# Batch 0's x moved to SyncE's queue, between pieces of w_in, and the first stage's order rewritten around it

## The chip, the cores and the metric

The kernel runs on one core of a Trainium2 chip. The metric is the device time of one execution in microseconds (us), as the median of several runs.

## The reference

Two blocks follow each other. The first is a cross attention between x (8 batches, 8 heads, 512 tokens, 64 channels) and a state (8, 8, 32, 64), in both directions; the second is a feed-forward layer on the 4352 resulting rows of 512 (8 batches of 512 + 32 tokens).

```python
scores = scale * np.matmul(x, state.transpose(0, 1, 3, 2))      # x reads state
a = softmax(scores); xread = np.matmul(a, state)
scores2 = scale * np.matmul(state, x.transpose(0, 1, 3, 2))     # state reads x
a2 = softmax(scores2); sread = np.matmul(a2, x)
x2 = rows of concat([xread, sread])                             # (4352, 512)
h = x2 @ w_in                                                   # w_in (512, 2048)
out = (h * sigmoid(1.702 * h)) @ w_out                          # w_out (2048, 512)
```

The softmax subtracts the maximum and divides by the sum plus 1e-9. x, state and out are 32-bit floats; w_in and w_out come as 64-bit floats, and the kernel itself makes 32-bit ones of them.

## The kernel before

The order of every instruction on each engine is written by hand: the program is under `manual_schedule`, and each engine works through its instructions in the order of the code. The change lies in the first stage, which brings in the data and handles batches 0 and 1; batches 2 to 7 follow in a different way and are not touched.

**Transfers.** The states of batches 0 and 1 come in two halves (`load_two_states`, L138, 64 KB each, issued from ScalarE's queue); a GpSimd copy makes a second arrangement of each half. `load_x(b)` (L150) brings one batch's x, 1 MB: batch 0's in four pieces of 256 KB from ScalarE's queue, batch 1's in two pieces of 512 KB from SyncE's queue, in rows of 1 KB. `load_weights(upto)` (L272) goes on with the list of weight pieces up to a number; a piece (`load_weight`, L185) is 512 KB of w_in or w_out as 64-bit words, in rows of 4 KB, always from SyncE's queue. Four pieces (NPR = 4) hold a quarter of w_in's columns.

**Making 32-bit weights.** For each piece, VectorE takes the exponent bits (`mask`, L217), two ScalarE activations turn these into a power (`round_a`, L224, driven by `powers_to`, L277), and VectorE takes the fraction (`fraction`, L236), puts the sign to the power (`sign`, L243) and finishes with two products (`round_b`, L248, driven by `round_to`, L283). `round_to(n, ahead)` brings the pieces below n to their end, and the masks and powers of `ahead` more.

**Attention of a batch.** `two_states(b, banks)` (L313) turns the states on TensorE into two PSUM banks and copies them on ScalarE into `pairs`, four copies of 64x128; `state_copies(b)` (L325) makes two further copies of 128x128. `xT_part(b, j)` (L338) turns a quarter of x, that is two heads, with four TensorE transposes and one ScalarE copy to SBUF. `x_scores(b, j, banks)` (L352) makes a quarter of the scores with eight matmuls, from the turned x and `pairs`. `head_max`, `head_sub` (L362, L369, VectorE), `head_exp` (L376, ScalarE), `head_sum` and `head_scale` (L380, L389, VectorE) are the softmax of x's direction; `head_back` (L395) turns its result with eight TensorE transposes, copied by ScalarE. `att_scores(b)` (L412) makes the scores of the other direction and needs the copies of `state_copies`. `att_M(b, c)` (L542) multiplies the states by a quarter of w_in, and `up_x` (L626) makes hidden units of that product and the turned softmax, with the gelu on ScalarE.

**Buffers.** `att_ps` gives a PSUM buffer from psA, of which there are two. `bank_o` are four banks by themselves; `held` is the last two of them, and `apart` two banks of psH. The turned x of the two batches shares one SBUF buffer, and `pairs` is one buffer too.

**Warm-up.** `keep_warm(n, bank)` (L129) issues n bf16 matmuls of 128x512 on zeros, which nothing reads; the result goes to a bank that is not in use then.

Of the kernel before, what the change touches and what calls it, by code (L numbers as in the profile page):

```python
# [10 lines left out]
FP32 = mybir.dt.float32  # L11
# [9 lines left out]
def kernel(  # L21
# [30 lines left out]
    nc = tc.nc  # L52
# [5 lines left out]
    P = 128  # L58
    NPR = P // Ns
    NG = H // NPR  # L60
# [3 lines left out]
    FC = 512  # L64
# [10 lines left out]
    x_four = x.rearrange("b h (q c) d -> b q h (c d)", c=SCH)  # L75
# [13 lines left out]
    psH = ctx.enter_context(tc.tile_pool(name="psH", bufs=2, space=bass.MemoryType.PSUM))  # L89
# [4 lines left out]
    def att_ps(shape, name):  # L94
        return psA.tile(shape, FP32, tag="att", name=name)
# [31 lines left out]
    bank_o = [psO.tile([P, FC], FP32, tag=f"o{i}", name=f"o_{i}") for i in range(4)]  # L127

    def keep_warm(n, bank=None):  # L129
        ps = psH.tile([P, FC], FP32, tag="h", name="warm") if bank is None else bank  # L130
        for _ in range(n):
            nc.tensor.matmul(ps, zeros[:, :P], zeros, start=True, stop=True)


    xn, xsq, stn = {}, {}, {}
    two = [konst.tile([P, 2, 2, D], FP32, name=f"states_{i}") for i in range(2)]

    def load_two_states():  # L138

        for u in range(2):  # L140
            nc.scalar.dma_start(two[0][:, :, u], st_h[:, :2, u])
        for u in range(2):
            nc.gpsimd.tensor_copy(two[1][:, :, 1 - u], two[0][:, :, u])
# [6 lines left out]
    def load_x(b):  # L150
        t = sums[:, 0] if b == 1 else xpool.tile([P, SCH, H, D], FP32, tag="xn", name=f"xn_{b}").rearrange("p c h d -> p (c h d)")
        xn[b] = t.rearrange("p (h c d) -> p h c d", h=H, c=SCH)
        n = NPR if b else NG
        for i in range(H // n):
            h = slice(n * i, n * (i + 1))
            (nc.sync if b else nc.scalar).dma_start(xn[b][:, h].rearrange("p h c d -> p h (c d)"), x_four[b, :, h])

    def load_x_squares(b):
        xsq[b] = xpool.tile([P, NPR, S], FP32, tag="xn", name=f"xsq_{b}")
# [25 lines left out]
    def load_weight(i):  # L185

        key = PIECES[i]
        nin, room = NFC * NPR, NF // 2
        if i < room or nin - NPR <= i < nin:
            o = 2 * (i % room if i < room else i - (nin - NPR))  # L190
            raw[i] = w_out[:, o : o + 2].rearrange("p f n -> p (f n)").bitcast(I32)
        else:
            o = 2 * (i % 4)
            raw[i] = later[:, o : o + 2].rearrange("p f n -> p (f n)").bitcast(I32)
        if key[0] == "i":
            _, c, k = key
            src = w_in_words[P * k : P * (k + 1), 2 * FC * c : 2 * FC * (c + 1)]
        else:
            src = w_out_words[P * key[1] : P * (key[1] + 1)]
        nc.sync.dma_start(raw[i], src)  # L200
# [23 lines left out]
    def round_a(i):  # L224

        if i not in power:
            mask(i)
        sc = power[i]
        if i in (NFC * NPR + 2, NFC * NPR + 3):
            nc.vector.tensor_scalar(sc, sc, most, least, ALU.min, ALU.max)  # L230
            nc.vector.tensor_scalar(sc, sc, -least, 8.0, ALU.add, ALU.mult)
            return
        nc.scalar.activation(out=sc.bitcast(FP32), in_=sc, func=AF.Relu, bias=edge[0], scale=-8.0)
        nc.scalar.activation(out=sc, in_=sc.bitcast(FP32), func=AF.Relu, bias=edge[1], scale=-1.0)
# [37 lines left out]
    def load_weights(upto):  # L272
        while done["load"] < min(upto, len(PIECES)):
            load_weight(done["load"])
            done["load"] += 1

    def powers_to(n):  # L277
        while done["a"] < min(n, len(PIECES)):
            load_weights(done["a"] + 1)
            round_a(done["a"])  # L280
            done["a"] += 1

    def round_to(n, ahead=AHEAD):  # L283

        nin = NFC * NPR
        while done["b"] < min(n, len(PIECES)):
            i = done["b"]
            powers_to(i + 1)
            round_b(i, min(i + 1 + ahead, i + 3 if i > nin + 3 else i + 2 if i >= nin else nin), i >= nin or i + 1 < nin and (i + 1 < n or i >= NPR))
            done["b"] += 1  # L290
            while done["b"] > NPR and done["load"] < len(PIECES) and before(done["load"]) < done["b"]:
                load_weights(done["load"] + 1)
# [20 lines left out]
    def two_states(b, banks):  # L313

        A[b]["turn"] = banks
        A[b]["two"] = [apool.tile([P, P], FP32, tag=f"two{i}", name=f"two{i}_{b}", bufs=2) for i in range(2)]
        for ps, t in zip(banks, two):
            nc.tensor.transpose(ps, t[:, b].rearrange("p u d -> p (u d)"), ident)
        for i in range(2):
            rows = slice(D * i, D * (i + 1))  # L320
            for u in range(2):
                src = banks[u ^ i][rows].rearrange("p (h n) -> p h n", n=Ns)
                nc.scalar.copy(pairs[rows, NPR * u : NPR * (u + 1), i], src)

    def state_copies(b):  # L325
        for t, ps in zip(A[b]["two"], A[b]["turn"]):
            nc.scalar.copy(t, ps)
# [24 lines left out]
    def x_scores(b, j, banks):  # L352

        ps = banks[j // 2].rearrange("p (c g j n) -> p c g j n", c=SCH, g=NG, n=Ns)[:, :, :, j % 2]
        for g in range(NG):
            for i in range(2):
                nc.tensor.matmul(
                    ps[:, 2 * i : 2 * i + 2, g], A[b]["xT"][:, NG * j + g, i], pairs[:, NG * j + g].rearrange("p i n -> p (i n)"),
                    start=True, stop=True,
                )  # L360
# [8 lines left out]
    def head_sub(b, i, banks):  # L369
        a = A[b]  # L370
        t = a["e1"][:, :, :, 2 * i : 2 * i + 2].rearrange("p c g j n -> p (c g) j n")
        ps = banks[i].rearrange("p (k j n) -> p k j n", j=2, n=Ns)
        mx = a["mx"][:, i].rearrange("p (k j) -> p k j", j=2)
        nc.vector.tensor_tensor(out=t, in0=ps, in1=mx.to_broadcast((P, SCH * NG, 2, Ns)), op=ALU.subtract)

    def head_exp(b):  # L376
        t = A[b]["e1"]
        nc.scalar.activation(out=t, in_=t, func=AF.Exp, scale=scale)
# [16 lines left out]
    def head_back(b, g, bank=None):  # L395

        a = A[b]
        if g == 0:
            a["aT"] = low[:, :NG] if b == 1 else apool.tile([P, NG, S], FP32, tag="aT", name=f"aT_{b}")
        ps = att_ps([P, SCH, P], f"aT_{b}_{g}") if bank is None else bank.rearrange("p (c q) -> p c q", c=SCH)  # L400
        for c in range(SCH):
            nc.tensor.transpose(ps[:, c], a["e1"][:, c, g].rearrange("p j n -> p (j n)"), ident)
        nc.scalar.copy(a["aT"][:, g], ps.rearrange("p c q -> p (c q)"))
# [8 lines left out]
    def att_scores(b):  # L412
        a = A[b]
        a["s"] = bank_o[:NG] if b == 0 else bank_o[NG:]
        if b > 1:
            by_state(b, a["s"], lambda rows, j: a["xT"][rows, j])
            return

        for g in range(NG):
            for j in range(NPR):  # L420
                st = slice(Ns * j, Ns * (j + 1))
                for i in range(2):
                    rows = slice(D * i, D * (i + 1))
                    nc.tensor.matmul(
                        a["s"][i][st, 2 * P * g : 2 * P * (g + 1)], state_of(b, NG * j + g, i),
                        a["xT"][rows, NG * j + g], start=True, stop=True,
                    )
# [827 lines left out]


    load_two_states()
    load_x(0)
    load_weights(NPR)
    load_x(1)  # L1260
    load_weights(2 * NPR)
    nc.scalar.activation(out=one, in_=one, func=AF.Exp)
    keep_warm(14)
    powers_to(1)
    fraction(0)
    powers_to(2)
    round_to(2, 0)
    two_states(0, [bank_o[i][:, :P] for i in range(2)])
    held, apart = bank_o[NG:], [psH.tile([P, FC], FP32, tag="h", name=f"apart_{i}") for i in range(2)]
    for j in range(NPR):  # L1270
        keep_warm(1, held[0])
        xT_part(0, j, apart[j - 2] if j > 1 else None)
    for j in range(NPR):
        x_scores(0, j, held)
# [5 lines left out]
    fraction(2)  # L1280
    head_max(0, 1, held)
    head_sub(0, 1, held)
    att_scores(0)
    two_states(1, [att_ps([P, P], f"two_{i}") for i in range(2)])
    state_copies(1)
    xT_part(1, 0)
    head_exp(0)
    keep_warm(1, held[0])
    xT_part(1, 1)
    x_scores(1, 0, apart)  # L1290
    xT_part(1, 2)
    x_scores(1, 1, apart)
    keep_warm(1, held[0])
    xT_part(1, 3)
    x_scores(1, 2, apart)
    round_to(3, 1)
    head_sum(0)
    mask(NPR)
    powers_to(NPR + 1)
    head_scale(0)  # L1300
    for g in range(NG):
        head_back(0, g)
    x_scores(1, 3, apart)
    keep_warm(2, held[0])
    round_to(NPR, 2)
    att_M(0, 0)
    for i in range(2):
# [349 lines left out]
```

## Time and profile before

| | |
|---|---|
| median of 3 runs | 696.64 us (696.45 to 696.75) |
| the profiled execution | 697.09 us |
| its span, first to last instruction | 695.3 us |
| PE busy | 684.9 us, 98% of the span |
| PE weight loads (PEld, beside the matmuls) | 585.3 us |
| VectorE (DVE) busy | 558.4 us, 80% |
| ScalarE (ACT) busy | 325.9 us, 47% |
| DMA from 3 to 28 us | 390 GB/s, 9.74 MB |
| first up_x | 30.8 us |
| granted TensorE clock, mean | 0.996 |

The span runs from the first instruction to the last; the profiled execution's own time lies 1.8 us over it. In the profile L12 means line 12 of the kernel, SPq and ACTq are the issues of transfers on the queues of SyncE and ScalarE, and "out<-in" are the program's buffers. Batch 0's x is `xn`, batch 1's is `sums`, and a piece of w_in arrives in `w_out` or `later`, whose room it borrows.

### The profile page before, as it was taken

To read this page: it belongs to the slowest core of one execution; us is meant where nothing else is said; L and a number is where in the kernel's file an instruction comes from. 1 tells how busy PE (TensorE), PEld (TensorE's weight loads), DVE (VectorE), ACT (ScalarE), POOL (GpSimd) and SP (SyncE) were. 2 spreads that over 40 slices of the span, in tenths; PEclk is the share of its full clock that TensorE was granted. 3 is DMA by queue.
4 is the path that set the end of the run, shared out by engine and by line. 5 is a ranking of instruction groups with operands and counts; after the bars stand their busy time and mean duration, and the time that the engine had idled before them with its cause. 6 is when DMAs were issued, how large, how long until landed. Compare 5 with 4: busy or idle time off the path is not lost.

```text
span 695.3 us, 13727 instructions
## 1 busy us (share of the span) xinstructions
PE 684.9 (98%) x5408; PEld 585.3 (84%) x5408; DVE 558.4 (80%) x1066; ACT 325.9 (47%) x728; POOL 1.9 (0%) x11
## 2 busy tenths in 40 slices
PE   8899999999999999999999999999999999999996
PEld 5543577778998899889988999989988998999995
DVE  4899898999999888788969796988788895886540
ACT  5788844224337523753355534643375236421410
POOL 1000000000000000000000000000000000000000
PEclk9999999999999999999999999999999999999999
DMA  9711336146534564346441755166424740251000
GB/s 323 290 61 62 122 122 140 46 175 194 194 74 127 167 191 147 64 129 194 150 95 48 229 166 114 29 182 203 120 46 138 212 138 16 76 166 46 4 2 29
DMA packets 100160, 87.41 MB, mean 126 GB/s; under 512 B 56576, under 2 KB 79616, under 8 KB 100096
## 3 DMA queue, kind: packets, MB, share of 16 engines
q1 hardware_dynamic: 98464, 85.35, 41.5%
q10 hardware_dynamic: 1632, 1.18, 0.5%
q8 instruction: 43, 0.70, 0.4%
q14 instruction: 21, 0.17, 0.1%
HBM read 68.94 MB, written 17.56 MB: 124 GB/s over the span
## 4 chain that ended last, share of the span: by engine, by line
PE 94%; ACT 3%; DMA 2%; ACTq 0%; DVE 0%; issue 0%; DVEq 0%
PE low L764 28%; PE o L1174 15%; PE o L764 15%; PE upx L1174 6%; PE h L621 5%; PE M L410 4%; PE o L1472 4%; PE down L1472 3%; PE o L663 2%; PE upw L1174 2%; PE o L813 2%; PE down_up L621 2%; DMA xn<-in_x_dram 1%; PE o L410 1%; PE upx_sr L1174 1%; DMA out_dram<-osb_sr 1%
## 5 line engine op out<-in xcount | busy, mean ns | idle before, releaser
L764 PE MATMUL low<-w_out,g_room 128*128 128x128 f32 x416 | 54.3, 276 | 0.0
L764 PEld LDWEIGHTS low<-w_out,g_room 128*128 128x128 f32 x416 | 50.5, 192 | 4.5 <-issue 4.2
L1174 PE MATMUL o<-ta,M 128*128 128x256 f32 x192 | 49.9, 382 | 0.0
L1174 PE MATMUL upx<-aT,M 128*128 128x256 f32 x192 | 49.3, 379 | 0.0
L764 PE MATMUL low<-low,g_room 128*128 128x128 f32 x336 | 43.3, 275 | 0.0
L1174 PEld LDWEIGHTS o<-ta,M 128*128 128x128 f32 x192 | 35.5, 190 | 6.0 <-ACT g_room L1220 1.6
L764 PEld LDWEIGHTS low<-low,g_room 128*128 128x128 f32 x336 | 40.3, 192 | 0.2 <-DVE later L769 0.2
L1174 PEld LDWEIGHTS upx<-aT,M 128*128 128x128 f32 x192 | 36.0, 190 | 4.6
L553 ACT COPY M<-M 128x512 f32<-128x512 f32 x57 | 29.7, 594 | 15.4 <-PE M L410 15.4
L1180 ACT ACTIVATE g_room<-o 128x512 f32<-128x512 f32 (+1 forms) x56 | 31.3, 560 | 10.4 <-PE o L1174 10.4
L764 PE MATMUL low<-sums,later 128*128 128x128 f32 x272 | 34.9, 275 | 0.0
L764 PEld LDWEIGHTS low<-sums,later 128*128 128x128 f32 x272 | 32.7, 192 | 0.1
L820 DVE TENSOR_TENSOR g_room<-g_room 128x512 f32<-128x512 f32 x48 | 31.7, 684 | 0.2
L1174 PE MATMUL o<-ta,ms 128*128 128x256 f32 x120 | 30.8, 379 | 0.0
L621 PE MATMUL h<-aT,M 128*128 128x512 f32 x64 | 28.9, 599 | 0.0
L1220 ACT COPY g_room<-o 128x512 f32<-128x512 f32 (+1 forms) x28 | 15.5, 555 | 25.4 <-PE o L1174 25.4
L1180 ACT ACTIVATE g_room<-g_room 128x512 f32<-128x512 f32 (+1 forms) x28 | 16.8, 600 | 20.8 <-DVE g_room L1183 20.8
L1174 PEld LDWEIGHTS o<-ta,ms 128*128 128x128 f32 x120 | 22.8, 190 | 3.1
L621 PEld LDWEIGHTS h<-aT,M 128*128 128x128 f32 x64 | 11.8, 190 | 15.8 <-issue 11.5
L1174 PE MATMUL o<-aT,m 128*128 128x256 f32 x96 | 24.6, 379 | 0.0
L764 PEld LDWEIGHTS o<-w_out,g_room 128*128 128x128 f32 x160 | 19.4, 192 | 5.0 <-issue 5.0
L410 PE MATMUL M<-w_in,stT 64*32 64x512 f32 x344 | 23.2, 592 | 0.0
(316 smaller groups left out, 1653.6 us busy)
## 6 DMA issues: line engine op xcount, KB each, us to landing
low<-low SPq DMA_DIRECT2D x108, 256.0 KB, 2.6
low<-low SPq DMA_DIRECT2D x11, 768.0 KB, 4.3
later<-in_moe_w_out_dram SPq DMA_DIRECT2D x16, 512.0 KB, 3.5
w_out<-in_moe_w_in_dram SPq DMA_DIRECT2D x12, 512.0 KB, 7.4
xsq<-in_x_dram SPq DMA_DIRECT2D x96, 64.0 KB, 2.3
xn<-in_x_dram SPq DMA_DIRECT2D x12, 512.0 KB, 4.4
out_dram<-osb SPq DMA_DIRECT2D x15, 256.0 KB, 2.2
out_dram<-later SPq DMA_DIRECT2D x14, 256.0 KB, 2.2
```

Of the source, the lines that this page charges most:

```text
L410: nc.tensor.matmul(ps[g][st], state_of(b, NG * j + g, g), rhs(rows, j), start=True, stop=True)
L553: nc.scalar.copy(m[:, g], ps[g])
L621: nc.tensor.matmul(hps, lhs[i], rhs[i], start=(i == 0), stop=(i == n - 1))
L663: nc.tensor.matmul(ps[:, r], lhs[f][:, P * r : P * (r + 1)], rhs[:, f], start=(first and r == 0 and f == 0), stop=(f == HF - 1), skip_grou ...
L764: nc.tensor.matmul(ps, lhs[f], rhs[:, f], start=(first and f == 0), stop=(f == QF - 1), skip_group_check=True)
L813: nc.tensor.matmul(ps[:, r], lhs[f][:, P * r : P * (r + 1)], rhs[:, f], start=(r == 0 and f == 0), stop=(f == HF - 1), skip_group_check=True,)
L820: nc.vector.tensor_tensor(out=out, in0=x0, in1=x1, op=op)
L1174: nc.tensor.matmul(ps[:, k], lhs[i][:, o : o + P], rhs[i], start=(first and k == 0 and i == 0), stop=(i == n - 1), skip_group_check=True,)
L1180: nc.scalar.activation(out=dst, in_=src, func=AF.Gelu_apprx_sigmoid)
L1220: nc.scalar.copy(c12, Y(u))
L1472: nc.tensor.matmul(ps7[name][:, HN * r : HN * (r + 1)], lhs[:, P * r : P * (r + 1)], rhs, start=(i == 0 and r == 0), stop=(i == HF - 1), s ...
```

## The change

All four pieces of batch 0's x are issued from SyncE's queue, after the first two pieces of w_in and before the third. Of the transfers of the first stage only the two of the states stay on ScalarE's queue. The warm-up at the start has 10 matmuls instead of 14, and `two_states(0)` is followed by two; the single warm-ups ahead of each turn of batch 0's x and those among batch 1's turns and scores go. Batch 1's states are turned and copied ahead of `att_scores(0)`, into the two `apart` banks instead of two buffers of psA. `head_exp(0)` comes ahead of the first turn of batch 1's x, and `powers_to(NPR + 1)` behind `head_back(0)`.

```diff
@@ load_x
-            (nc.sync if b else nc.scalar).dma_start(xn[b][:, h].rearrange("p h c d -> p h (c d)"), x_four[b, :, h])
+            nc.sync.dma_start(xn[b][:, h].rearrange("p h c d -> p h (c d)"), x_four[b, :, h])
@@ the first stage
     load_two_states()
+    load_weights(2)
     load_x(0)
     load_weights(NPR)
     load_x(1)
     load_weights(2 * NPR)
     nc.scalar.activation(out=one, in_=one, func=AF.Exp)
-    keep_warm(14)
+    keep_warm(10)
     powers_to(1)
     fraction(0)
     powers_to(2)
     round_to(2, 0)
+    held, apart = bank_o[NG:], [psH.tile([P, FC], FP32, tag="h", name=f"apart_{i}") for i in range(2)]
     two_states(0, [bank_o[i][:, :P] for i in range(2)])
-    held, apart = bank_o[NG:], [psH.tile([P, FC], FP32, tag="h", name=f"apart_{i}") for i in range(2)]
+    keep_warm(2, held[0])
     for j in range(NPR):
-        keep_warm(1, held[0])
         xT_part(0, j, apart[j - 2] if j > 1 else None)
     for j in range(NPR):
         x_scores(0, j, held)
@@
     head_max(0, 1, held)
     head_sub(0, 1, held)
+    two_states(1, [apart[i][:, :P] for i in range(2)])
+    state_copies(1)
     att_scores(0)
-    two_states(1, [att_ps([P, P], f"two_{i}") for i in range(2)])
-    state_copies(1)
+    head_exp(0)
     xT_part(1, 0)
-    head_exp(0)
-    keep_warm(1, held[0])
     xT_part(1, 1)
     x_scores(1, 0, apart)
     xT_part(1, 2)
     x_scores(1, 1, apart)
-    keep_warm(1, held[0])
     xT_part(1, 3)
     x_scores(1, 2, apart)
     round_to(3, 1)
     head_sum(0)
     mask(NPR)
-    powers_to(NPR + 1)
     head_scale(0)
     for g in range(NG):
         head_back(0, g)
+    powers_to(NPR + 1)
     x_scores(1, 3, apart)
-    keep_warm(2, held[0])
     round_to(NPR, 2)
     att_M(0, 0)
```

## The prediction

> **What bounds the kernel now.** I read the chain that ended last first: 94% of it is PE, and in order of time it shows no wait worth a change after 30.9 us, so what can be won at the start lies ahead of that.
>
> ```profile
> 2.26 7.92 DMA xn<-in_x_dram
> 10.22 1.11 PE xT L349 x4
> 11.78 1.11 PE apart L349 x4
> 13.32 0.66 PE apart L349 x4
> 13.97 3.52 PE o L357 x32
> 17.49 1.02 PE o L424 x32
> 18.82 0.42 ACT low L323 x2
> 20.00 0.66 PE xT L349 x4
> 24.56 0.59 ACT xT L350
> 30.88 5.35 PE h L621 x12
> ```
>
> The columns are start, length and what. Batch 0's x is awaited until 10.2, its last pieces keep PE until 14.0, its scores end at 17.4; then batch 1's states pass through ScalarE, then batch 1's x, and at 24.6 the chain changes to ScalarE, which works without a pause up to the first copy of M at 30.1. From 30.8 PE runs on. Next the stretches (core 0; PE, PEld, DVE, ACT, POOL busy, granted clock, DMA share, GB/s):
>
> ```profile
> 0.00:5.00 5.00, 3.81 (x9) 1.35 (x10) 0.28 (x2) 0.00 (x0) 1.24 (x9) 1.00 0.61 188
> 5.00:8.00 3.00, 2.48 (x8) 0.82 (x7) 1.28 (x3) 2.13 (x4) 0.67 (x2) 1.00 1.04 378
> 8.00:9.00 1.00, 0.47 (x3) 0.09 (x3) 0.28 (x1) 1.00 (x2) 0.00 (x0) 1.00 1.11 358
> 10.20:13.60 3.40, 3.37 (x13) 2.28 (x14) 2.99 (x6) 2.31 (x7) 0.00 (x0) 0.50 1.08 355
> 3.00:28.00 25.00, 22.07 (x159) 15.21 (x157) 16.09 (x30) 16.11 (x34) 0.67 (x2) 0.93 1.04 390
> ```
>
> From 3 to 28 us the DMA engines are full at 390 GB/s: nothing arrives sooner unless something else arrives later. So order of arrival is what counts. And PE had half its clock from 10.2 to 13.6. The waits of SyncE's queue and its timeline give the landings:
>
> ```profile
> SPq L156 <- DMA states<-in_state_dram: 2.0, 1, 2.0
> SPq L200 <- DMA xn<-in_x_dram: 1.8, 3, 1.2
> 7.54 0.38 SPq L156 DMA_DIRECT2D sums<-in_x_dram  x1
> 12.93 0.33 SPq L200 DMA_DIRECT2D later<-in_moe_w_in_dram  x1
> ```
>
> [...] batch 1's first x at 7.54 with the second states, the next at 8.97 with the first x of batch 0, then at 10.20, 11.75 and 12.93 with its second to fourth. PE's turns start with these (8.99, 10.22, 11.78, 13.11). Batch 1's two x pieces land by 14.01 and 15.51 in the same way. The first two weight pieces land at 5.19 and 6.71, where VectorE's masks begin.
>
> [...] x, behind the states on ScalarE's queue, lands between pieces of w_in, 1.2 to 1.6 us apart. [...] Here it changes at about 6.8, 10.2 and 13.6. [...] the stretch before 13.6 held 12 turns and two or three warm-up matmuls, and full clock followed.
>
> **The change part by part.**
>
> *x of batch 0 moves to SyncE's queue behind two pieces of w_in.* Ahead of and with its last piece are then 0.13 MB of states, 1.05 MB of w_in and 1.05 MB of x: 2.23 MB. By the stretches the engines had moved 5 x 188 = 0.94 MB at 5 us, 2.07 MB at 8 and 2.43 at 9, so 2.23 MB at about 8.45. Landing lags: by 6.71 about 1.58 MB had moved, while the landed pieces are 1.1 MB, some 1.1 us less. Last piece 8.45 + 1.1 = 9.6 us instead of 12.9; the others at 0.26 MB over 376 GB/s = 0.7 us: 7.4, 8.1, 8.85. Bounds 9.0 to 10.5[...]. Issue costs little: SyncE takes about 0.4 us for each, all six by 3 to 5 us, well before the data can flow. [...]
>
> *What comes later for it.* w_in's third piece lands at 9.6 + 0.52 MB/0.39 = 11.0 (before, about 8.4 at the earliest, used at 12.8 by VectorE), the fourth at 12.3, batch 1's x at 13.8 and 15.3, as before, the same bytes being ahead. VectorE's rounding of the first two pieces ends near 11.2: it used to wait for ScalarE until 8.72, since ScalarE, held by its issues until 5.7, loaded its table at 5.77. Now that load is over by 3.3 and the first power runs at 5.7, not 7.2. So the mask of the third piece (0.42 us) is not held up, and ScalarE's powers of it end at about 13.4.
>
> *States.* [...] second half at 7.0 (bounds 6.5 and 7.54), plus POOL's copy of 0.30: PE turns them at 7.35.
>
> *Warm-up.* 14 took 5.96 us, 0.43 each, thus half clock; 10 end at 1.19 + 4.27 = 5.5. With windows as before, the one ending at 6.8 is then busy for 60%; that from -0.0 to 3.4 was busy 65% and brought no full clock, so PE stays at half. States 0.43, two warm-ups 0.85: 8.65. Turns of x at 4 x 0.21 = 0.85: 9.5, 10.3. The window 6.8 to 10.2 is busy for 2.9 of 3.4 us, 84%[...]. I take full clock at 10.2: turns three and four at 0.45 each end at 11.2. Scores 3.57 (13.81 to 17.38): **14.8 instead of 17.4**, 2.6 us won. ScalarE's four copies of states (0.21 each) and first copies of x fit under these turns.
>
> *Batch 1's states ahead of att_scores, exp ahead of the first copy, no warm-ups.* With S the end of scores: before, turning the states waited for att_scores (0.9), their copies ended at S + 2.6 (20.0), and the turn of x had to wait for their PSUM buffers (1.35), so that scores(1,0) began at S + 3.96. After: states turned at S + 0.3, six copies of 0.21 to S + 1.6; exp needs max and sub of the second half on VectorE (2 x 0.7) and ends at S + 2.6; x's turns have run beside it; its copy 0.55: scores(1,0) at S + 3.2. The copies, scores (0.9) and turns (0.45) that alternate then reach the fourth copy at S + 6.15, against 24.56 - 17.38 = 7.2: **1.0 won**. What waits behind the exp is that copy and PE's scores; they are in this sum.
>
> *powers_to(NPR + 1) behind head_back.* Two activations, 1.4 us, trade places with two copies of aT. From the fourth copy to M, ScalarE has the same sum (three pairs of 1.4, two copies of 0.47), 5.6 us: no gain there, but att_M starts 1.4 earlier and has slack. VectorE's third rounding, which att_M needs, ends after its 0.33 mask, sign, two products (0.6 each) behind the power: about 24.9, before M's copy at 26.6.
>
> Sum: 2.6 + 1.0 = 3.6 us, the first up_x at 27.2. After it, VectorE must follow: at 45.6 it had piece 7 ready (44.2 + 0.69) 0.7 us ahead of PE. Its third rounding moves from 28.9 to 24.9, so it keeps pace. The profiled execution took 697.09 us (span 695.3, 1.8 around it), 0.45 over the median of 696.64; so 693.5 profiled, **693.1 as median**.
>
> **Rivals.**
> 1. *Clock already full when x comes* (windows lying otherwise, one inside the warm-ups): turns limited by landing, 9.6 + 0.6, scores end at 13.8; 4.6 won, 692.0. [...] Against: ten warm-ups span 4.3 us, so a window of 3.4 fits only in a quarter of the positions.
> 2. *Clock full only at 13.6*: 84% did not suffice. Turns end at 12.05, scores do 1.6 us of work at half rate, S = 16.3; 2.1 won, 694.5.
> 3. [...] the gain is given back: x lands no sooner in effect, because its slowest engine lags or VectorE's third rounding slips by 2 to 3 us behind w_in's later pieces, and PE waits at 45.6. Only batch 1's part is left, 1.0 or less: 696.0. Against: 2.2 MB ahead instead of over 3.
> 4. *Slower: the missing warm-ups cost the clock.* If PE counts turns badly, neither 10.2 nor 13.6 nor 17.05 raises it: scores take 7.1 us, S = 19.2, 1.8 late; what follows until 20.5 runs at half as well (0.9 more), less the 1.0: 698.4. It decides where full clock comes after about 17.6 us. Against: the trace's raise at 13.6 after mostly turns, and scores are plain matmuls.
>
> **Numbers.** Likeliest case 0.58, rival 1 0.13, 2 0.15, 3 0.08, 4 0.06. Cases one to three are faster by over 0.2% (1.4 us, about what a measurement of this kernel can tell from no change): 0.86; same 0.08; slower 0.06. The likeliest case with x between 9.0 and 10.5 gives 692.4 to 694.2; the range reaches to rivals 1 and 2: 691.8 to 695.2.
>
> **What would show it.** Right: the last turn of x starting near 10.5, scores ending near 15, batch 1's state copies before att_scores ends, the first up_x near 27.2, no new PE wait at the second att_M. Wrong: turns waiting for DMA beyond 11, a half clock while the scores run, VectorE idle for w_in's third piece, or an up_x start won and lost again before 62 us.

## The result, and the profile after

The changed kernel takes **692.87 us** (median of 4 runs, 692.59 to 693.3) against 696.69 before, measured beside it: ratio 0.9946, 95% interval 0.9929 to 0.9963. The forecast was 693.1 with a range of 691.8 to 695.2. The profiled execution took 692.59 us with a span of 690.8; before, 697.09 and 695.3. The profile of before lies 0.4 us above its median and that of the changed kernel 0.3 below, so the two profiles differ by 4.5 us and the medians by 3.8.

The chain of waits of the changed kernel, its first 31 us (start, length, what):

```profile
3.04 6.06 DMA xn<-in_x_dram
...
9.15 0.67 PE apart L349 x4
9.82 0.11 issue
9.93 0.63 PE apart L349 x4
10.56 3.54 PE o L357 x32
...
15.56 1.06 ACT e L378
16.62 0.48 ACT xT L350
17.11 0.04 issue
17.15 1.10 PE apart L357 x8
...
20.02 0.59 ACT xT L350
...
23.67 0.70 DVE w_in L263
24.38 0.04 issue
24.42 0.62 PE M L410 x2
...
26.33 4.92 PE h L621 x11
```

x of batch 0 is still what the chain starts from, but its third piece lands at 9.1 instead of 11.75, the fourth turn starts at 9.9 instead of 13.1, and the scores run from 10.4. Between them and batch 1's first scores at 17.15 now stand VectorE's maximum and subtraction and ScalarE's exp, and the states of batch 1 have left the chain. Further on the way has changed too: before, ScalarE led without a pause to the first copy of M, and now VectorE's rounding of w_in's fourth piece (the prediction's third rounding), which ends at 24.4, is what att_M waits for (0.36 us). ScalarE is no freer for it: it works without a pause from 20.02 to M's copy at 25.6, and both ways end within some 0.2 us of each other. The first up_x comes 4.5 us sooner (26.3 against 30.8), and PE then works without a wait worth naming, so that the end moves by the same 4.5 us between these two executions.

The stretches of the changed kernel (PE, PEld, DVE, ACT, POOL busy, granted clock, DMA share, GB/s):

```profile
2.26:5.67 3.41, 3.37 (x8) 0.91 (x6) 0.55 (x2) 0.98 (x3) 0.34 (x1) 1.00 0.94 322
5.67:9.09 3.42, 1.90 (x12) 1.33 (x12) 2.61 (x6) 3.28 (x7) 0.32 (x2) 1.00 1.11 349
10.20:13.60 3.40, 3.40 (x34) 3.40 (x32) 2.77 (x5) 3.00 (x7) 0.00 (x0) 1.00 1.05 373
3.00:28.00 25.00, 22.10 (x185) 14.69 (x184) 20.36 (x38) 19.23 (x41) 0.66 (x2) 1.00 1.04 388
```

The DMA engines are as full from 3 to 28 us as before (388 against 390 GB/s): nearly the same bytes in another order. In the same 25 us VectorE is busy for 20.4 instead of 16.1 us and ScalarE for 19.2 instead of 16.1: the work that used to follow has moved in. And the clock from 10.2 to 13.6 is 1.00, not 0.50. In the kernel before, the trace has the granted clock change at 6.81, 10.22 and 13.64, 3.41 us apart; a window means here a stretch of that length from one such place to the next. In this execution full clock began at 5.67, behind a window in which warm-ups kept PE busy for 3.37 us of 3.41 (its line shows 1.00 only because the trace has no record of the clock before its end), and lasted, though PE was busy for only 1.90 us (56%) of the next window.

A wait of SyncE's own queue, changed kernel (waited for: us in total, times, longest):

```profile
SPq L156 <- DMA states<-in_state_dram: 0.9, 1, 0.9
```

Batch 1's x still waits for the second half of the states, but 0.9 us instead of 2.0: it is issued at 7.07, not 7.54. The DMA engines stay full meanwhile (349 GB/s from 5.67 to 9.09).

### The profile page after: what moved, and what is told of

The parts are those of the page before. It is cut to its first block, busy times and chain, and to the rows that moved or that the text cites. A ratio compares the mean times of both kernels' runs of the same rounds, so it can differ in the third digit from the quotient of the medians.

```text
span 690.8 us, 13707 instructions
## 1 busy us (share of the span) xinstructions
PE 680.8 (99%) x5398; PEld 583.5 (84%) x5398; DVE 558.6 (81%) x1066; ACT 325.7 (47%) x728; POOL 1.9 (0%) x11
## 4 chain that ended last, share of the span: by engine, by line
PE 94%; ACT 2%; DMA 2%; DVE 1%; SPq 0%; issue 0%; DVEq 0%
PE low L764 28%; PE o L1174 15%; PE o L764 15%; PE upx L1174 6%; PE h L621 5%; PE M L410 4%; PE o L1470 4%; PE down L1470 3%; PE o L663 3%; PE upw L1174 2%; PE o L813 2%; PE down_up L621 2%; PE o L410 1%; PE upx_sr L1174 1%; DMA out_dram<-osb_sr 1%; PE sr L595 1%
## 5 line engine op out<-in xcount | busy, mean ns | idle before, releaser
L764 PEld LDWEIGHTS low<-low,g_room 128*128 128x128 f32 x336 | 40.3, 192 | 0.2 <-DVE later L769 0.2
L1180 ACT ACTIVATE g_room<-o 128x512 f32<-128x512 f32 (+1 forms) x56 | 31.3, 559 | 10.4 <-PE o L1174 10.4
L1174 PE MATMUL o<-ta,ms 128*128 128x256 f32 x120 | 30.8, 379 | 0.0
## 6 DMA issues: line engine op xcount, KB each, us to landing
w_out<-in_moe_w_in_dram SPq DMA_DIRECT2D x12, 512.0 KB, 10.2
```

Of the source, the lines that this page charges most:

```text
L764: nc.tensor.matmul(ps, lhs[f], rhs[:, f], start=(first and f == 0), stop=(f == QF - 1), skip_group_check=True)
L1174: nc.tensor.matmul(ps[:, k], lhs[i][:, o : o + P], rhs[i], start=(first and k == 0 and i == 0), stop=(i == n - 1), skip_group_check=True,)
L1180: nc.scalar.activation(out=dst, in_=src, func=AF.Gelu_apprx_sigmoid)
```

## The experiments

Theory: x's place in the order of arrival carries some 3 us, batch 1's rewritten order some 1 us, and the clock decides how much of the first is seen. Rivals: the warm-ups carry the gain; the landing of x alone decides; scores raise the clock by themselves.

**The changed kernel again** (no edit), to see its spread.

> The changed kernel once more, to see how its times spread. If the clock at the start is a matter of where the clock's windows lie (theory), its times fall between 692.4 and 694.0, those with full clock from the warm-ups near 692.6 and those with full clock only from 9 to 10 us near 693.3, and the profile may show either. If the spread of the first four runs (0.7 us) was chance of the measurement alone (rival), the times lie as close together as those of the kernel before, within 0.4 us.

Measured: 693.48 (692.80 to 693.79, 5 runs), ratio 0.9952 (0.9940 to 0.9964). Two runs lie at 692.80 and 692.85, three at 693.48 to 693.79; with the four of the first measurement, four of nine lie at or below 692.85, five from 693.11 up, and the median of the nine is 693.11. The mean granted clock goes with it: 0.998 in the four, 0.996 or 0.997 in the five. The profile fell into the upper group. Its stretches between the clock's changes (4.05, 7.46 and 10.88), and its chain:

```profile
0.64:4.05 3.41, 2.86 (x7) 1.03 (x8) 0.28 (x2) 1.49 (x2) 1.03 (x5) 1.00 0.55 152
4.05:7.46 3.41, 1.08 (x5) 0.34 (x3) 1.43 (x4) 1.63 (x3) 0.66 (x2) 1.00 1.08 371
7.46:10.88 3.42, 3.42 (x15) 2.83 (x15) 3.38 (x7) 2.83 (x8) 0.00 (x0) 0.50 1.06 380
```

```profile
8.84 1.71 PE xT L349 x8
10.55 1.09 PE apart L349 x8
11.64 3.54 PE o L357 x32
```

The first stretch was at half clock too, whatever its 1.00 says (its warm-ups take 0.43 us each, those at full clock 0.21); full clock began at 4.05, after a window that was busy for 2.86 of 3.41 us, 84%. It was lost after the next one (1.08 of 3.41), in which the ten warm-ups had run out and the states weren't there, and came back at 10.88. The first eight turns of x take 1.9 us in the timeline, against 1.0 in the first profile, and the scores end 1.1 us later. (The end of the scores, S, is taken here as the start of the next matmul.) For x and the scores that is the case that the prediction called likeliest (S = 14.8, here 15.0); the first profile is its rival 1 (13.8, there 13.9). In these two traces the groups are two places of full clock. Both had it while warm-ups ran (from 5.67 and from 4.05); in one it lasted until x came, in the other it was lost at 7.46 and came back at 10.88.

**The transfers alone.**

```diff
     load_two_states()
+    load_weights(2)
     load_x(0)
...
-            (nc.sync if b else nc.scalar).dma_start(xn[b]...
+            nc.sync.dma_start(xn[b]...
```

> The kernel before with the transfer edit alone: x of batch 0 on SyncE's queue behind two pieces of w_in; warm-ups, batch 1's states, exp and powers as before. Theory (arrival decides): x's last piece lands near 9.8, scores end near 14.1 instead of 17.4, all that follows comes 3.3 us sooner: 693.4. Rival (the clock, that is the new warm-ups, carries the gain): under 1 us, above 695.7. Rival (the rest of the order is what makes use of it): gain between, as batch 1's x lands no sooner.

Measured: 693.63 (693.47 to 693.73), ratio 0.9957 (0.9945 to 0.9968): 3.0 us won. Scores start at 10.45, at full clock (3.68 us), the first up_x at 27.45. So the transfers make up most of the gain, with the old warm-ups; the rival that these carry it falls. Batch 1's part is as it was: turns wait 1.1 us for the states' copies (PE xT L349 <- ACT two L327).

**Batch 1's order alone**, x on ScalarE's queue, 14 warm-ups and one ahead of each turn of batch 0's x:

```diff
     head_sub(0, 1, held)
+    two_states(1, [apart[i][:, :P] for i in range(2)])
+    state_copies(1)
     att_scores(0)
-    two_states(1, [att_ps([P, P], f"two_{i}") for i in range(2)])
-    state_copies(1)
+    head_exp(0)
     xT_part(1, 0)
-    head_exp(0)
... (the rest of the change from here on as it stands)
```

> The changed kernel's order behind batch 0's softmax alone (states of batch 1 ahead of att_scores, exp ahead of the first turn, no warm-ups there, powers behind head_back); x of batch 0 on ScalarE's queue and the warm-ups at the start as in the kernel before. Theory: scores end at 17.4 as before and the fourth copy of batch 1's x comes 1.0 us sooner: 695.7. Rival: the parts overlap, DMA or VectorE binds in between, and it is within 0.3 of before, 696.4 or more.

Measured: 695.68 over 21 runs, ratio 0.9988 (0.9981 to 0.9996): 0.9 us won, as expected. One of the 21 runs took 700.29 with a lower mean clock (0.992). The two parts sum to 3.9 us; the whole change brought 3.8 and 3.1 in its two measurements. With 14 warm-ups, below, it brought 4.2, so that having only 10 is probably what costs the rest.

**All of the change but the earlier x**: the new order and the new warm-ups, x on ScalarE's queue.

```diff
-    load_weights(2)
     load_x(0)
...
-            nc.sync.dma_start(xn[b]...
+            (nc.sync if b else nc.scalar).dma_start(xn[b]...
```

> The changed kernel with x of batch 0 on ScalarE's queue ahead of the pieces of w_in, as before: all of the new order and the new warm-ups, without the earlier x. Theory: x arrives at 9.0 to 12.9, the turns stand alone without warm-ups between them and keep PE busy for some 65% of a window, which does not raise the clock before 13.6 to 17; part or all of the scores run at half, ending 1 to 1.7 us later than before, less the 1.0 of batch 1's part: 696.5 to 697.5, no faster than before, and the half clock shows in the trace while the scores run. Rival: warm-ups don't matter and it is as fast as batch 1's part alone, 695.7.

Measured: **699.8**, ratio 1.0029 (1.0012 to 1.0045), slower than before; four of 14 runs at 695.15 to 695.85, as fast as batch 1's order alone, ten at 699.5 to 700.7. The trace shows the half clock for 13.65 us:

```profile
13.64 6.93 PE L357 MATMUL o<-low,xT 128*128 128x64 f32 x32
```

```profile
2.96:6.38 3.42, 2.68 (x7) 0.67 (x5) 0.85 (x2) 0.88 (x1) 0.37 (x1) 1.00 1.01 372
...
9.79:13.20 3.41, 2.67 (x10) 1.90 (x11) 3.13 (x6) 2.41 (x7) 0.00 (x0) 0.50 1.07 356
13.20:16.62 3.42, 3.42 (x19) 3.42 (x17) 0.00 (x0) 2.27 (x6) 0.00 (x0) 0.50 1.07 391
16.62:20.03 3.41, 3.41 (x18) 3.41 (x17) 1.72 (x3) 0.00 (x0) 0.00 (x0) 0.50 1.03 410
20.03:23.44 3.41, 3.41 (x40) 1.86 (x40) 2.80 (x5) 2.29 (x7) 0.00 (x0) 0.50 1.02 407
```

The clock rose first at 6.38, behind a window that warm-ups filled to 78% (2.68 us). (The first line shows 1.00 for the reason given above.) It was lost at 9.79, and the next window, filled to the same 78% (2.67 us) by turns of x alone, left it at half. The scores took 6.93 us instead of 3.68, and behind two whole windows, 13.2 to 20.0, in which PE shows as busy without a gap (3.42 and 3.41 us), it was still at half. It rose at 23.4 after a window with the end of the scores, att_scores and turns. I had expected full clock by 17 us and 696.5 to 697.5: in ten of 14 runs it was worse. This kernel and the one with batch 1's order alone differ in the warm-ups only. So with x late the missing warm-ups cost 4.1 us in the median (699.8 against 695.68), and the trace shows the half clock with it; with the earlier x the change does without them (692.87).

**Fourteen warm-ups at the start** of the changed kernel:

```diff
-    keep_warm(10)
+    keep_warm(14)
```

> The changed kernel with 14 warm-ups at the start instead of 10. They span 6.0 us at half clock, so that one of the clock's windows of 3.4 us lies within them nearly always. Theory (the two groups of times are two places of full clock): full clock from the warm-ups in all runs, times 692.5 to 692.9 within 0.3, the upper group near 693.5 gone. Rival (the groups have another cause, such as the landings): two groups as before, median 692.9 to 693.5. No run should be slower for the four more: the states aren't there before 7.05.

Measured: 692.52 (692.12 to 692.89), ratio 0.9938 (0.9926 to 0.9951). No run of the upper group is left (mean clock 0.998 to 1.000 in all five), the clock rises at 6.2, the states are turned at 7.09, no later than with ten. The spread (0.8 us) is wider than I expected; first up_x at 26.24 as in the first profile, which took 0.3 us less in all, so some of it arises later.

**Two warm-ups at the start.**

```diff
-    keep_warm(10)
+    keep_warm(2)
```

> The changed kernel with 2 warm-ups at the start instead of 10: no window is filled before the states come. What is left to raise the clock are two warm-ups and 16 turns, 7.2 to 12 us. Theory (turns raise the clock, scores don't, as two whole windows full of scores left it at half where x came late): two groups again, one near 693.5 to 694.3, where a window ends between some 10 and 12 us, and one with the scores wholly at half clock, 3.5 us later, near 696.5 to 697.5. Rival (scores raise it too): all within 693.3 to 695. Rival (turns don't): all near 697.

Measured: 694.31 (694.04 to 694.48), one group. Full clock came at 12.66 in the trace; the scores, from 11.88, ran 0.8 us at half and took 4.06 us. The second group did not show; these five runs don't tell whether scores raise the clock, as the window ahead of 12.66 held turns for most of it.

**No warm-up at all** (both `keep_warm` calls of batch 0 taken out of the changed kernel):

> The changed kernel without any warm-up, neither the 10 nor the 2. PE's work before the scores is then two turns of states and 16 of x, 7.2 to 11 us at half clock, then scores. Theory (turns raise the clock, scores don't): only a window that ends near 10.6 to 11.5 is filled by turns; otherwise scores run wholly at half, 3.6 us later than with full clock, and att_scores behind them at half too: most runs 697 to 698.5, some near 693.5. Rival (scores count as work for the clock): full clock at the latest where the first window after 7.2 is full, 10.6 to 14 us: all runs 693.3 to 695.2.

Measured: 693.4 over ten runs: seven at 692.79 to 693.58, three at 696.5 to 697.6. A second group at the expected place, but the smaller one: the theory had most runs there. In the trace full clock came at 12.45, after a window (busy for 3.41 us) of turns until 11.07 and scores from then: turns for some 60% of it, with scores for the rest, went ahead of a rise, where turns alone for 78% had not (9.79 to 13.20 above), nor had scores alone (13.20 to 20.03). What scores add to turns was not measured by itself.

**Batch 1's states behind att_scores**, with 14 warm-ups:

```diff
-    two_states(1, [apart[i][:, :P] for i in range(2)])
-    state_copies(1)
     att_scores(0)
+    two_states(1, [att_ps([P, P], f"two_{i}") for i in range(2)])
+    state_copies(1)
```

> The changed kernel with 14 warm-ups and batch 1's states turned after att_scores(0), in two buffers of psA as before. Theory: copies end 1.0 us later and the exp and the first copy of x with them: scores(1,0) at S + 4.2 instead of S + 3.2 (S: end of batch 0's scores), 1.0 us slower than 14 warm-ups alone, 693.7. Rival (exp and VectorE's sub set the time, the states are beside them): under 0.3 slower.

Measured: 693.54 (693.17 to 693.97), 1.0 slower than 14 warm-ups alone. The timeline of PE in it:

```profile
16.69 1.09 PE L349 MATMUL xT<-ident,sums 128*128 128x128 f32 x8 [1.11 <-ACT two L327]
18.29 1.10 PE L357 MATMUL apart<-low,xT 128*128 128x64 f32 x8 [0.51 <-ACT xT L350]
```

The turns again wait for the states' copies to give back their PSUM buffers. In this kernel the whole of batch 1's gain hangs on this move, of place and banks together; the two were not tried apart.

**exp behind the first turn of batch 1's x**, with 14 warm-ups:

```diff
-    head_exp(0)
     xT_part(1, 0)
+    head_exp(0)
```

> The changed kernel with 14 warm-ups and head_exp(0) behind the first turn and copy of batch 1's x, as before. In the changed kernel's trace scores(1,0) wait 0.8 us for that copy, which stands behind the exp. Theory: it comes before the exp, scores(1,0) at S + 2.4 instead of S + 3.2; the fourth copy and ScalarE's third power 0.6 to 0.8 sooner, first up_x as much: 692.0. Rival: the exp ends 0.5 later and VectorE's sum with it, so that VectorE's third rounding sets att_M and nothing is won: 692.5 to 692.8.

Measured: 692.21 (691.85 to 692.52), 0.3 less than without, with ranges that overlap; ratio to before 0.9933 (0.9921 to 0.9946). ScalarE's timeline shows why the trace itself gains more:

```profile
15.75 0.59 ACT L350 COPY xT<-xT 128x512 f32<-128x512 f32 x1 [0.42 <-PE xT L349]
16.23 1.06 ACT L378 ACTIVATE e<-e 128x1024 f32<-128x1024 f32 x1
```

The copy comes first, scores(1,0) start at 16.39, the first up_x at 25.69 instead of 26.24. Of these 0.55 us, 0.18 were there already at the end of batch 0's scores (13.72 against 13.90). So in the changed kernel the exp's new place seems to cost 0.3 to 0.4 us of what the states' new place wins; with ranges that overlap, two traces and five runs make this likely, not certain.

**x between the first and the second piece of w_in**, with 14 warm-ups:

```diff
-    load_weights(2)
+    load_weights(1)
     load_x(0)
```

> The changed kernel with 14 warm-ups and x of batch 0 one piece further ahead, between the first and the second piece of w_in. Theory (the place between second and third is where x and the rounding's start meet): x's last piece lands near 8.4 instead of 9.8, but the second piece of w_in at 9.8 instead of 6.7; ScalarE makes its power before it copies the states that the scores need, so scores begin near 12.6 instead of 10.4: some 2 us slower than 14 warm-ups alone, 694 to 695. Rival (x's arrival alone decides): 1.3 us faster, 691.2.

Measured: **699.26** (698.02 to 700.22), ratio 1.0032 (1.0019 to 1.0044). The timeline of PE:

```profile
8.07 1.13 PE L349 MATMUL apart<-ident,xn 128*128 128x128 f32 x8
13.08 7.09 PE L357 MATMUL o<-low,xT 128*128 128x64 f32 x32 [3.88 <-ACT xT L350]
```

x's turns are over at 9.2, but the second piece of w_in lands at 9.73, and ScalarE makes its power before it copies states and turned x: scores begin at 13.08, 0.5 later than expected. PE did nothing from 9.26 to 12.67, the clock fell to half at 12.67, and the scores took 7.09 us. The direction was right; the larger part of the loss, 3.4 us in the scores alone, is the clock, which the expectation had left out.

**ScalarE's and VectorE's ways to the first up_x shortened**, on top of 14 warm-ups and the later exp: `round_to(3, 1)` ahead of `xT_part(1, 3)`, `powers_to(NPR + 1)` behind `att_M(0, 0)`, `mask(NPR)` ahead of `head_scale(0)` taken out, no mask or power ahead in `round_to(NPR, 0)`, `powers_to(NPR + 2)` behind `sign(NPR)`.

> 14 warm-ups, exp behind the first turn of batch 1's x, and in addition the third piece's power ahead of the fourth copy of x, the masks and powers of the fifth and sixth piece behind att_M(0, 0) and sign. It takes from VectorE's way to the end of the third rounding two masks (0.7 us) and the wait for the power (0.3 to 0.7), and from ScalarE's way to M two pairs of activations (2.8 us). Theory (first up_x is set by these two ways): first up_x near 24.3 instead of 25.7 and, as VectorE itself gains only some 0.5, a new wait of 0.2 to 0.5 us at the second att_M: 691.2. Rival (all of it is lost again by VectorE, which has the same work to do before piece 7): 692.2 as without.

Measured: 691.94 (691.71 to 692.17), ratio 0.9927 (0.9914 to 0.9940), the lowest median here, 0.3 under the one with the later exp alone, with ranges that overlap. The first up_x comes at 24.89, 0.8 sooner, but batch 1's first up_x at 33.27 instead of 33.54: the gain is given back ahead of it. The waits of PE's loads from 28 to 36 us:

```profile
PEld h L621 <- ACT low L403: 1.1, 2, 0.9
```

The copies of batch 1's turned softmax come late, as the moved power and the gelus stand before them on ScalarE. The place of the new wait that I had named, the second att_M, was wrong.

## Why the prediction was right, point by point

- **Order of arrival under a full DMA: right.** x's last two pieces were forecast for 8.85 and 9.6; the turns that start with them start at 9.15 and 9.93. Part of the difference is a slip: 1.58 MB moved against 1.1 landed, at 378 GB/s, is a lag of 1.3 us, not 1.1. The states were turned at 7.18 (7.35 forecast), w_in's third piece was masked at 11.34 (11.2), its power ended at 13.3 (13.4), and the bandwidth was nearly the same with x on the other queue (388 against 390 GB/s from 3 to 28 us). The first users start in the order of issue: w_in's first two pieces are masked at 5.12 and 6.68, x is turned from 8.04 to 10.4, w_in's third piece is masked at 11.34. The transfers alone bring 3.0 us.
- **The clock at the start: the weights were wrong.** Five of nine runs lie where the likeliest case puts them, four of nine in rival 1's place, which had been given 0.13. The failing step is "a window fits only in a quarter of the positions": that asked for a wholly filled window. In the traces full clock followed a window that warm-ups filled to 84% (it ended at 4.05) and one filled to 78% (it ended at 6.38); behind one filled to 65% (0 to 3.4 in the kernel before, 2.21 us) the warm-ups went on at 0.43 us each, at half clock. Rises from 4.05 to 6.38 would be two thirds of the positions of a window of 3.41 us, an estimate from these two ends. But a rise isn't enough, and what the prediction did not price is its loss before x comes: the clock was lost after a window busy for 32% (upper group) and kept after one busy for 56% (lower group). The kernel before lost it after one busy for 59% (6.81 to 10.22), so the busy share alone does not decide. That 84% would do at 10.2 was the author's estimate: in the kernel before, both rises came behind stretches that were busy nearly throughout (3.41 of 3.41 us up to 6.81, 3.37 of 3.40 up to 13.6).
- **The number: the range is right for its stated reasons, the closeness is luck.** 693.1 was the forecast of the likeliest case alone. Runs of that kind took 693.11 to 693.79, and those of rival 1 692.59 to 692.85 (692.0 forecast), so each case came out less fast than forecast. The median of 692.87 lies between the groups, where no run was. One reason may be the profile that the prediction started from: its mean clock was 0.996, while 29 of 35 later executions of the same kernel have 0.998 or more. The half clock from 10.2 to 13.6 was then probably an exception, and part of what was won there is missing in the medians.
- **Batch 1's part: right.** Forecast scores(1,0) at S + 3.2 and the fourth copy at S + 6.15; with S = 13.9, measured 17.15 and 20.02, S + 3.2 and S + 6.1. Alone it brings 0.9 us. The states' move is all of it; the exp's move, which the sum took as part of the gain, seems to take 0.3 to 0.4 us back.
- **The first up_x** was forecast at S + 12.4; 26.26 is S + 12.4. The way there was only half foreseen. ScalarE's sum is right (5.6 us from the fourth copy to M's; the parts listed for it make 5.1, the rest is the fourth copy itself). But att_M was to have slack, and it waits for VectorE's third rounding, which ends at S + 10.5 instead of S + 10.1. That this cost next to nothing is luck: ScalarE's way is just as long. After the first up_x the span has 664.5 us in both profiles (695.3 - 30.81, 690.8 - 26.26): nothing was given back. VectorE's piece 7 was ready at 40.3, 0.7 ahead of the second att_M at 41.06, the same slack as before.
- **Rival 4, the clock lost through missing warm-ups, did not come about, but other runs had such a loss.** The reason set against it, "scores are plain matmuls", fell: behind two windows full of scores (13.20 to 20.03, all of the change but the earlier x) the clock was still at half. With x late, or with PE idle for a window ahead of the scores (9.26 to 12.67), this turns a gain into some 3 us of loss (699.8 and 699.26). Turns, too, went ahead of full clock: from 7.46 to 10.88 PE, busy for 3.42 us, had two warm-ups, and for the rest turns, and the clock rose. But turns alone for 2.67 us of a window left it at half, in the trace where it had risen behind warm-ups for 2.68 us of a window.
- **What stays open:** what in PE's work decides the clock. It rose behind windows of 512-wide warm-ups (2.68 to 3.37 us of 3.41, three traces) and behind one of turns and two warm-ups (3.42 us); it didn't behind two of 128x64 scores with a weight load each (3.42 and 3.41 us). Whether that goes with the width or with the share of weight loads was not tried apart, and the ends of matmuls in a trace are modelled, so that the busy shares are rough. The place of `powers_to(NPR + 1)` was not tried alone.

## What to carry to other kernels

Where the DMA engines are full from the start, as here (390 GB/s before, 388 after, from 3 to 28 us), a load is made sooner by putting it ahead of another, so ask for each what its first user could do without it; here w_in's third piece, masked at 11.34 and needed only behind the rounding of the first two, came later at no cost, and x one piece further ahead cost 6.7 us, more than half of it through the clock. Behind such a stage, follow the chain through every engine to the point from which one engine runs alone: here time won ahead of it was kept to the end. And before taking warm-up matmuls away, look in the trace at what PE does in the 3.4 us ahead of the long small matmuls (here 3.68 us of scores became 6.93 at half clock), and at single runs, since an average over them hides two places of the clock (four of nine runs and five of nine here).

## What the runs showed that I had not expected

In two traces a busy PE stayed at half clock: with 32 score matmuls of 128x64 over two windows of 3.41 us without a gap (13.20 to 20.03), and again from 12.67 to 19.49 with x one piece further ahead (busy for 3.00 and 3.41 us), and the scores took 6.93 and 7.09 us instead of 3.68. In the kernel before, where full clock had come at 13.64, the same matmuls ran at it, and the window of the end of the turns and of scores (13.64 to 17.05) was followed by full clock. The two windows of the kernel before, the one ahead of the loss at 10.22 and the one behind the return at 13.64:

```profile
6.81:10.22 3.41, 2.02 (x10) 0.78 (x8) 1.83 (x4) 3.27 (x8) 0.30 (x1) 1.00 1.07 374
13.64:17.05 3.41, 3.41 (x33) 3.41 (x31) 1.27 (x2) 2.25 (x5) 0.00 (x0) 1.00 1.05 398
```

Full clock followed windows 78% and 84% full of 512-wide bf16 matmuls (2.68 us up to 6.38, 2.86 up to 4.05); half clock followed one with PE idle throughout (0.00 us, 9.26 to 12.67).
